# Grouping the small matrix products of a recurrent attention block, and lagging the values by half a unit

## The chip, the cores and the metric

The kernel runs on one core of one Trainium2 chip. The metric is the device time of the whole kernel in microseconds (us), from the first to the last instruction with what lies around them. All data are float32.

## The reference

A gated linear recurrence over 768 steps, for 4 batches and 8 heads of 48 channels, feeds a two-layer network with an ELU between its layers.

```python
mag = np.sqrt(a_re * a_re + a_im * a_im)
scale = np.minimum(mag, 0.999) / (mag + 1e-06)
a_re_n, a_im_n = (a_re * scale, a_im * scale)
for t in range(S):
    new_re = ar * S_re - ai * S_im
    new_im = ar * S_im + ai * S_re
    S_re, S_im = (new_re + kv, new_im)       # kv: outer product of k[t] and v[t]
    y[:, :, t] = einsum('bhd,bhde->bhe', q[:, :, t], S_re)
# x: y as (B*S, H*D) = (3072, 384)
h = x @ w_in                                  # 384 -> 2048
g = where(h > 0, h, exp(min(h, 0)) - 1)
out = g @ w_out                               # 2048 -> 384
```

## The kernel before: units, queues and a list written out by hand

The work is cut into 12 **units** (u = 0 to 11). A unit is 128 time steps of two batches; the two batches are its **halves** (n = 0, 1). Units u and u + 2 carry the same two batches on, so the state of one goes into the other. Inside a half the 128 steps are two chunks of 64.

A unit goes through these stages, each a function of the source:

- **Gates.** `squares`, `joined`, `logarithms`, `powers`, `lengths`, `ratios`, `slopes`, `angles`, `carried`, `noted` turn a_re and a_im into log magnitudes and angles on ScalarE (ACT), VectorE (DVE) and GpSimd (POOL). `decays` (`quartered`, L883) sums the logs over a chunk on TensorE (PE) and ACT takes six exponentials of them (L893). `turns` (L832) sums the angles on PE, four DVE operations (L837, L840) take off whole turns, `waves` makes sine and cosine with three ACT operations (L962, L965, L966), `scaled` multiplies q and k by the decays, `ends` fetches the chunk totals, and `gated` (L988) writes the gated q (DVE) and the gated k (POOL).
- **Small products.** For each half: `transposed` q and k (L1003 on PE, L1004 copies on ACT), `scores` (L1011, masked on DVE by L1016), `states` (L1039, then L1049 on DVE and L1051 on POOL for the running state), `values` (scores times v, L1061, then the carried state times q, L1068, then copies on ACT, L1076 and L1080). `seam` moves the rest of the values into place with DMAs of POOL's queue (L1093).
- **First layer.** `inner` (L1113) makes 256 columns of h in six products, which the trace shows as 12 matmuls of 128x128 by 256. `elu` follows: Relu (L1122) and Exp (L1123) on ACT, then L1124 on DVE. There are eight of each pair in a unit, written f = 0, 2, ... 14.
- **Second layer.** From unit 2 on it is 14 `product` calls (L1219, eight matmuls by 192 columns in the trace), a form of Strassen's scheme. `folded` (L1197, four DVE operations for each half of g) makes the combinations of g that it takes.

[...]

What sets the order: the code runs under a manual schedule. Each engine issues its instructions in the order in which the functions are called, and that is a list. The list `first` is written out to the end of unit 3 and some of unit 4's gates (down to `powers`, 4). After it come the calls made by `put(at, function, ...)`, sorted by `at`, and for equal `at` by the order in which they were put, that is by unit. A unit has SLOTS = 16 slots, and r = 16 (u - 2). Before the change, unit u loads at r + 8, has its gates from r + 11 to r + 19.5, its small products from r + 22 to r + 31, its eight `inner`/`elu` from r + 36 to r + 43 and its products from r + 44 to r + 52. So the gates and small products of unit u stand between the large products of units u - 1 and u - 2. A call that is in `first` already is not repeated. SP's queue issues the loads, the output stores and, every four slots, a `test_fetch` of weights (a DVE `test`, L680, follows it).

Of the kernel before, what the change touches and what calls it, by code (L numbers as in the profile page):

```python
# [10 lines left out]
FP32 = mybir.dt.float32  # L11
U32 = mybir.dt.uint32
AF = mybir.ActivationFunctionType
ALU = mybir.AluOpType
PSUM = bass.MemoryType.PSUM

C = 128
L = 64
# [487 lines left out]
def kernel(  # L506
# [12 lines left out]
    nc = tc.nc  # L519
    B, H, S, D = q.shape  # L520
    DM, DF = moe_w_in.shape[0], moe_w_out.shape[0]
    NI, NF = DM // C, DF // C
    NP = H // 2
    HD = H * D
    NB = 2
    NU = B // NB * (S // C)
# [10 lines left out]
    ps = ctx.enter_context(tc.tile_pool(name="ps", bufs=1, space=PSUM))  # L537
# [10 lines left out]
    def const(n, m, name):  # L548
        return cst.tile([n, m], FP32, name=name)
# [8 lines left out]
    G = HP - D  # L558
# [12 lines left out]
    def work(shape, tag="w"):  # L571
        return ps.tile(shape, FP32, tag=tag, bufs=3, name=tag)


    nat = [{} for _ in range(NU)]

    def where(u):
        return u % (B // NB) * NB, u // (B // NB) * C
# [107 lines left out]
    def flat(t):  # L686
        return t.rearrange("p n h d -> p (n h d)")
# [5 lines left out]
    def new(tag, bufs=1, shape=None):  # L693
        return sb.tile(shape or [C, NB, H, D], FP32, tag=tag, bufs=bufs, name=tag)
# [182 lines left out]
    def quartered(u):  # L877

        x = nat[u]
        both = [work([C, HD]) for n in range(NB)]  # L880
        for c in range(C // L):
            for n, t in enumerate(both):
                nc.tensor.matmul(  # L883
                    t[ts(c ^ n, L)], lhsT=sum_logs[ts(c, L), ts(c, L)],
                    rhs=flat(x["l"][ts(c, L), n : n + 1]), start=True, stop=True,
                )
        for n, t in enumerate(both):
            for key, sign in (("E", 1.0), ("F", -1.0)):
                pairs = [(slice(0, C), slice(0, C))]
                if n:  # L890
                    pairs = [(ts(c, L), ts(1 - c, L)) for c in range(C // L)]
                for to, of in pairs:
                    nc.scalar.activation(  # L893
                        out=flat(x[key][to, n : n + 1]), in_=t[of], func=AF.Exp, scale=sign
                    )
        ends = dram.tile([NB, C // L, H, D], FP32, tag="ends", bufs=2, name="ends")
        nc.scalar.dma_start(
            out=ends.rearrange("n c h d -> c n (h d)"),
            in_=x["E"][L - 1 :: L].rearrange("p n h d -> p n (h d)"),
        )  # L900
        x["ends"] = ends
# [11 lines left out]
    def decays(u):  # L913
        x = nat[u]
        if u > 1:
            x["E"], x["F"] = new("n", 6), new("n", 6)
            quartered(u)
            return
        for n in range(NB):
            x["sums", n] = work([C, HD])  # L920
            nc.tensor.matmul(
                x["sums", n], lhsT=sum_logs, rhs=x["l"][:, n].rearrange("p h d -> p (h d)"),
                start=True, stop=True,
            )
            decayed(u, n)
# [68 lines left out]
    state = {}  # L994
# [23 lines left out]
        )  # L1018

    def states(u, n):  # L1020

        x = nat[u]
        b, s = where(u)
        x["S", n] = [state.get(b + n)]
        if s == S - C:
            last = C // L - 1
        else:
            last = C // L
        gs = [
            work([C, H, D], "w" if u else "mlp") for c in range(last)  # L1030
        ]
        for h in range(H):
            for c, g in enumerate(gs):
                k = gates["k"][ts(c, L), n, h]
                parts = [(g[ts(i, HP), h], k[:, i]) for i in range(2)]
                if u == 0:
                    parts = [(g[:, h], k.rearrange("p i d -> p (i d)"))]
                for to, of in parts:
                    nc.tensor.matmul(  # L1039
                        to, lhsT=of, rhs=vn[u % 2][ts(c, L), n, ts(h, D)], start=True, stop=True,  # L1040
                    )
        for c, g in enumerate(gs):
            old = x["S", n][-1]
            new_s = new("S", 8, [C, H, D])
            wide = x["T"][:, n, c].unsqueeze(2).to_broadcast([C, H, D])
            if old is None:
                nc.vector.tensor_tensor(out=new_s, in0=g, in1=wide, op=ALU.mult)
            else:
                nc.vector.tensor_tensor(out=new_s, in0=g, in1=old, op=ALU.add)  # L1049
                eng = nc.vector if u < 2 else nc.gpsimd  # L1050
                eng.tensor_tensor(out=new_s, in0=new_s, in1=wide, op=ALU.mult)  # L1051
            x["S", n].append(new_s)
        state[b + n] = x["S", n][-1]

    def values(u, n):
        x = nat[u]
        y = ps.tile([C, C // L, 512], FP32, tag="y", bufs=1, name="y")
        each = [(p, c, j) for p in range(NP) for c in range(C // L) for j in range(2)]
        for p, c, j in each:

            nc.tensor.matmul(  # L1061
                y[ts(j, HP), c, ts(p, L)], lhsT=vn[u % 2][ts(c, L), n, ds((2 * p + j) * D, HP)],
                rhs=x["a", n][ts(c, L), 2 * p + j], start=(p == 0), stop=False,
                skip_group_check=True,
            )
        for p, c, j in each:
            if x["S", n][c] is not None:
                nc.tensor.matmul(  # L1068
                    y[ds(j * HP, D), c, ts(p, L)], lhsT=x["S", n][c][:, 2 * p + j],
                    rhs=x["qt", n][:, 2 * p + j, ts(c, L)], start=False, stop=False,  # L1070
                    skip_group_check=True,
                )
        if n == 0:
            x["x"], x["y"] = new("x", 2, [C, NI, GT]), new("y", 1, [C, GT])

        nc.scalar.copy(  # L1076
            out=x["x"][:, :, ts(n, C)].rearrange("p x (c t) -> p c x t", c=C // L),
            in_=y[:, :, 0 : NI * L].rearrange("p c (x t) -> p c x t", x=NI),
        )
        nc.scalar.copy(  # L1080
            out=x["y"][:, ts(n, C)].rearrange("p (c t) -> p c t", c=C // L),
            in_=y[:, :, NI * L : NP * L],
        )

    def seam(u):

# [166 lines left out]
    def verdict():  # L1253
# [31 lines left out]
        out=ident, in_=ident, pattern=[[-1, C]], base=0, channel_multiplier=1,  # L1285
# [6 lines left out]
    sum_turns, mask = const(C, C, "sum_turns"), const(C, L, "mask")  # L1292
# [35 lines left out]
    def put(at, fn, *args):  # L1328
        if fn is hidden:
            plan.append((at, len(plan), inner, args))  # L1330
            plan.append((at, len(plan), elu, args))
        else:
            plan.append((at, len(plan), fn, args))

    def decays_of(u, *at):
        fns = squares, logarithms, powers, lengths, ratios, slopes, noted, angles, carried
        put(at[0], begun, u)
        for x, fn in zip(at, fns):
            put(x, fn, u)
            if fn is squares:  # L1340
                put(x, joined, u)

    def gates_of(u, *at):
        for x, fn in zip(at, (decays, turns, waves, scaled, ends, gated)):
            put(x, fn, u)

    def values_of(u, *at):
        fns = (transposed, "q"), (transposed, "k"), (scores,), (states,), (values,)
        for n in range(NB):
            for x, (fn, *key) in zip(at[5 * n :], fns):  # L1350
                put(x, fn, u, *key, n)
        put(at[-1], seam, u)
# [72 lines left out]

    for u in range(2, NU):
        r = (u - 2) * SLOTS
        put(r + 8, load_a, u)
        put(r + 8, load_v, u)
        put(r + 8, load_qk, u)  # L1430
        if u == 2:
            decays_of(u, 16, 17, 17, 18.4, 19.5, 19.6, 22.7, 19.8, 19.8)
            gates_of(u, 20.4, 21.6, 22.1, 22.4, 22.4, 22.6)
        else:
            decays_of(u, r + 11, r + 12, r + 12, r + 13.4, r + 13.5, r + 14.9, r + 16.7, r + 15.5, r + 16.6)
            gates_of(u, r + 15, r + 18, r + 18.5, r + 18, r + 18, r + 19.5)
        values_of(u, *(max(r + 22, 24.5) + x for x in (0, 1, 2, 3, 5, 4, 5, 6, 7, 8, 9)))
        layer_of(u, range(r + 36, r + 44), range(r + 44, r + 52))
    for m in range(NR):
        put(40 + 4 * m, test_fetch, m)  # L1440
# [1 line left out]
    put(NU * SLOTS, verdict)  # L1442
    items = [(fn, tuple(args)) for fn, *args in first]
    items += [x[2:] for x in sorted(plan, key=lambda x: x[:2]) if x[2:] not in items]
    for fn, args in items:
        fn(*args)
    ctx.close()
# [35 lines left out]
```

## Time and profile before

| what | us |
|---|---|
| median of 3 runs | 699.82 (699.59 to 703.32) |
| span of the profiled execution | 700.0 |
| TensorE matmul busy | 674.0 |
| TensorE weight loads busy | 580.5 |
| ACT busy | 398.5 |
| DVE busy | 389.3 |
| POOL busy | 197.3 |

From about 216 us on PE shows no wait, and one unit follows another every 53.49 us (the first `inner` of a unit starts at 335.43, 388.91 and 442.40 us). In a timeline a line gives the start of a run of like instructions, its length, engine, line, operation, what is written from what, shape and count; the idle time before it and what ended that stand in brackets. The ends of matmuls are modelled and overlap the next line, so lengths on PE are read from start to start.

### The profile page before, as it was taken

To read this page: it belongs to the slowest core of one execution; us is meant where nothing else is said; L and a number is where in the kernel's file an instruction comes from. 1 tells how busy PE (TensorE), PEld (TensorE's weight loads), DVE (VectorE), ACT (ScalarE), POOL (GpSimd) and SP (SyncE) were. 2 spreads that over 40 slices of the span, in tenths; PEclk is the share of its full clock that TensorE was granted. 3 is DMA by queue.
4 is the path that set the end of the run, shared out by engine and by line. 5 is a ranking of instruction groups with operands and counts; after the bars stand their busy time and mean duration, and the time that the engine had idled before them with its cause. 6 is when DMAs were issued, how large, how long until landed. Compare 5 with 4: busy or idle time off the path is not lost.

```text
span 700.0 us, 15771 instructions
## 1 busy us (share of the span) xinstructions
PE 674.0 (96%) x6656; PEld 580.5 (83%) x6656; DVE 389.3 (56%) x579; ACT 398.5 (57%) x630; POOL 197.3 (28%) x207
## 2 busy tenths in 40 slices
PE   8799899997999999999999999999999999999996
PEld 6687786575788889888988989889888988989995
DVE  5888999814757544554553553553554644642151
ACT  6774445748656764765655656657557547541230
POOL 2000000115514414414415415406407305402000
PEclk9979999999999999999999999999999999999999
DMA  9995756152082911821921821831731631100000
GB/s 169 175 150 83 144 176 165 17 103 64 3 137 63 143 50 38 138 43 50 136 48 53 123 61 52 121 63 53 108 75 53 123 62 52 47 1 8 23 1 28
DMA packets 149899, 55.98 MB, mean 80 GB/s; under 512 B 129172, under 2 KB 142652, under 8 KB 149820
## 3 DMA queue, kind: packets, MB, share of 16 engines
q1 hardware_dynamic: 146240, 53.53, 40.6%
q0 software_dynamic: 3360, 1.22, 1.3%
q8 instruction: 54, 0.88, 0.5%
q14 instruction: 25, 0.20, 0.1%
q10 hardware_dynamic: 220, 0.14, 0.1%
HBM read 48.88 MB, written 4.78 MB: 77 GB/s over the span
## 4 chain that ended last, share of the span: by engine, by line
PE 85%; DVE 4%; SPq 3%; ACT 2%; DMA 2%; issue 2%; POOL 1%; ACTq 0%; POOLq 0%; DVEq 0%
PE mlp L1113 33%; PE mlp L1219 26%; PE w L1003 5%; PE mlp L1134 4%; PE w L1011 3%; PE y L1068 3%; PE w L1039 3%; SPq L596 2%; PE y L1061 2%; PE w L832 2%; PE w L1134 1%; PE w L883 1%; DMA w<-in_moe_w_in_dram 1%; DMA w<-in_a_im_dram 1%; POOL kg L988 1%
## 5 line engine op out<-in xcount | busy, mean ns | idle before, releaser
L1113 PE MATMUL mlp<-x,w_in 128*128 128x256 f32 x1152 | 262.9, 383 | 2.9 <-DVE g L1124 2.9
L1113 PEld LDWEIGHTS mlp<-x,w_in 128*128 128x128 f32 x1152 | 215.8, 191 | 32.5 <-DVE g L1124 3.3
L1124 DVE SCALAR_TENSOR_TENSOR g<-ee,mlp 128x512 f32<-128x512 f32 x96 | 65.6, 685 | 116.6 <-ACT ee L1123 111.0
L1122 ACT ACTIVATE ee<-mlp 128x512 f32<-128x512 f32 x96 | 57.3, 596 | 127.6 <-PE mlp L1113 118.7
L1219 PE MATMUL mlp<-w_out,g 128*128 128x192 f32 x640 | 111.1, 328 | 0.0
L1219 PEld LDWEIGHTS mlp<-w_out,g 128*128 128x128 f32 x640 | 104.3, 190 | 2.8
L1051 POOL TENSOR_TENSOR S<-S,T 128x384 f32<-128x384 f32 x36 | 29.9, 831 | 163.7 <-DVE S L1049 163.7
L1123 ACT ACTIVATE ee<-ee 128x512 f32<-128x512 f32 x96 | 60.5, 630 | 2.9
L1197 DVE TENSOR_TENSOR g<-g 128x512 f32<-128x512 f32 x80 | 56.8, 711 | 2.7
L1219 PE MATMUL mlp<-w,g 128*128 128x192 f32 x320 | 56.9, 332 | 0.0
L1219 PEld LDWEIGHTS mlp<-w,g 128*128 128x128 f32 x320 | 51.6, 190 | 5.8 <-issue 4.8
L856 POOL DMA_DIRECT2D carry<-n x10 | 5.0, 501 | 142.0 <-DVE n L840 142.0
L988 POOL TENSOR_TENSOR kg<-k,cs 128x1536 f32<-128x1536 f32 x9 | 38.8, 4309 | 18.4 <-issue 18.4
L1093 POOL DMA_DIRECT2D x<-y x65 | 31.8, 496 | 42.7 <-ACT y L1080 42.7
L1049 DVE TENSOR_TENSOR S<-w,S 128x384 f32<-128x384 f32 x38 | 21.1, 556 | 40.7 <-PE w L1039 25.4
L893 ACT ACTIVATE n<-w 64x384 f32<-64x384 f32 (+1 forms) x60 | 28.1, 486 | 22.7 <-PE w L883 22.0
L1238 ACT COPY o<-mlp 128x192 f32<-128x192 f32 x10 | 3.2, 319 | 64.6 <-DMA out_dram<-o 42.9
L716 POOL TENSOR_TENSOR n<-n 128x768 f32<-128x768 f32 x9 | 16.4, 1819 | 66.9 <-ACT n L710 66.9
L1134 PE MATMUL mlp<-w_out,g 128*128 128x384 f32 x96 | 32.9, 490 | 0.7 <-DVE g L1124 0.7
L1004 ACT COPY qt<-w 128x512 f32<-128x512 f32 x48 | 25.5, 584 | 11.9 <-PE w L1003 11.9
L1011 PEld LDWEIGHTS w<-qt,kt 128*64 128x64 f32 x768 | 24.4, 137 | 7.9 <-issue 4.5
L988 DVE TENSOR_TENSOR qg<-q,cs 128x1536 f32<-128x1536 f32 (+1 forms) x12 | 19.5, 1623 | 19.2 <-ACT cs L966 19.2
(165 smaller groups left out, 992.3 us busy)
## 6 DMA issues: line engine op xcount, KB each, us to landing
w<-in_moe_w_out_dram SPq DMA_DIRECT2D x8, 768.0 KB
g<-in_moe_w_in_dram SPq DMA_DIRECT2D x16, 384.0 KB
g<-in_moe_w_out_dram SPq DMA_DIRECT2D x16, 384.0 KB
w<-in_moe_w_in_dram SPq DMA_DIRECT2D x16, 288.0 KB
vn<-in_v_dram SPq DMA_DIRECT2D x24, 192.0 KB
out_dram<-o SPq DMA_DIRECT2D x48, 96.0 KB
ar<-in_a_re_dram SPq DMA_DIRECT2D x22, 192.0 KB
ai<-in_a_im_dram SPq DMA_DIRECT2D x22, 192.0 KB
```

The source lines that it names most:

```text
L988: eng.tensor_tensor(out=to[:, :, :, 0:D], in0=each.unsqueeze(2).to_broadcast([C, step * H, 2, D]), in1=x["cs"][:, n * H : (n + step) * H], ...
L1003: nc.tensor.transpose(t[:, h], of, ident)
L1011: nc.tensor.matmul(t[ts(c, L), h], lhsT=x["kt", n][:, h, ts(c, L)], rhs=x["qt", n][:, h, ts(c, L)], start=True, stop=True,)
L1051: eng.tensor_tensor(out=new_s, in0=new_s, in1=wide, op=ALU.mult)
L1093: eng.dma_start(out=x["x"][ds(j * HP + D, G), i], in_=x["y"][ds(j * HP + i * G, G)])
L1113: nc.tensor.matmul(t[:, e], lhsT=w_in[:, i, ts(f + e, C)], rhs=x["x"][:, i], start=(i == 0), stop=(i == NI - 1),)
L1122: nc.scalar.activation(out=e, in_=t, func=AF.Relu, scale=-1.0)
L1123: nc.scalar.activation(out=e, in_=e, func=AF.Exp, scale=-1.0)
L1124: nc.vector.scalar_tensor_tensor(out=x["g", f // 8][:, f % 8 : f % 8 + 2], in0=e, scalar=-1.0, in1=t, op0=ALU.add, op1=ALU.max)
L1134: nc.tensor.matmul(x["o", n], lhsT=x["g", f // 8][:, f % 8, ts(n, C)], rhs=w_out[:, f], start=(f == 0), stop=(f == NF - 1),)
L1197: nc.vector.tensor_tensor(out=S_of(u, k, h), in0=a, in1=b, op=op)
L1219: nc.tensor.matmul(to, lhsT=a[:, m], rhs=b[:, m], start=(first and h == 0 and m == 0), stop=False, skip_group_check=True,)
```

## The change

From unit 4 on (`LONE = 4`):

- `states` and `values` are cut into their products and the rest (`state_products`, `state_sums`, `value_products`, `carried_products`, `value_copies`); the instructions are the same.
- `piece(u, n)` issues as one run: the log sums of unit u + 1 (for n = 1), value products of the half before, state products of this half, carried products of the half before, and scores of this half. After that come the state sums, the value copies of the half before and the mask of the scores.
- The scores are written to columns 256 to 511 of the two "y" banks, whose first 256 columns hold the values. One of the two banks of the log sums comes from "mlp" for u > 4.
- A unit's loads of a, q and k and its gates stand 8.5 slots earlier, its transposes and small products likewise: transposes from r + 13.5 and r + 21.2, pieces at r + 17 and r + 24.7. The values of n = 1 come with the first piece of the next unit, at r + 33, and `seam` after it. The first layer stays at r + 36.

```diff
-        both = [work([C, HD]) for n in range(NB)]
+        both = [work([C, HD], "mlp" if n and u > LONE else "w") for n in range(NB)]
...
+    LONE = 4
+
+    def piece(u, n):
+
+        u0, n0 = (u, 0) if n else (u - 1, 1)
+        half = H // 2
+        x = nat[u] if u < NU else None
+        if n and u + 1 < NU:
+            decays(u + 1)
+        y = ps.tile([C, C // L, 512], FP32, tag="y", bufs=1, name="y")
+        if u0 >= LONE:
+            value_products(u0, n0, y)
+        if x:
+            state_products(u, n)
+        if u0 >= LONE:
+            carried_products(u0, n0, y)
+        if x:
+            for h in range(H):
+                for c in range(C // L):
+                    nc.tensor.matmul(
+                        y[ts(c, L), h // half, ds(256 + h % half * L, L)],
+                        lhsT=x["kt", n][:, h, ts(c, L)], rhs=x["qt", n][:, h, ts(c, L)],
+                        start=True, stop=True, skip_group_check=True,
+                    )
+            state_sums(u, n)
+        if u0 >= LONE:
+            value_copies(u0, n0, y)
+        if x:
+            x["a", n] = new("a", 2, [C, H, L])
+            shape = [C, 2, half, L]
+            nc.vector.tensor_tensor(
+                out=x["a", n].rearrange("p (z h) t -> p z h t", z=2),
+                in0=y[:, :, 256:512].rearrange("p z (h t) -> p z h t", t=L),
+                in1=mask.unsqueeze(1).unsqueeze(1).to_broadcast(shape), op=ALU.mult,
+            )
...
     def gates_of(u, *at):
         for x, fn in zip(at, (decays, turns, waves, scaled, ends, gated)):
-            put(x, fn, u)
+            if fn is not decays or u <= LONE:
+                put(x, fn, u)
...
-        put(r + 8, load_a, u)
-        put(r + 8, load_v, u)
-        put(r + 8, load_qk, u)
+        b = r if u < LONE else r - 8.5
+        put(b + 8, load_a, u)
+        put(r + 8 if u < LONE else r + 4, load_v, u)
+        put(b + 8, load_qk, u)
...
-            decays_of(u, r + 11, r + 12, r + 12, r + 13.4, r + 13.5, r + 14.9, r + 16.7, r + 15.5, r + 16.6)
-            gates_of(u, r + 15, r + 18, r + 18.5, r + 18, r + 18, r + 19.5)
-        values_of(u, *(max(r + 22, 24.5) + x for x in (0, 1, 2, 3, 5, 4, 5, 6, 7, 8, 9)))
+            decays_of(u, b + 11, b + 12, b + 12, b + 13.4, b + 13.5, b + 14.9, b + 16.7, b + 15.5, b + 16.6)
+            gates_of(u, b + 15, b + 18, b + 18.5, b + 18, b + 18, b + 19.5)
+        if u < LONE:
+            values_of(u, *(max(r + 22, 24.5) + x for x in (0, 1, 2, 3, 5, 4, 5, 6, 7, 8, 9)))
+        else:
+            for n, at in enumerate((r + 13.5, r + 21.2)):
+                put(at, transposed, u, "q", n)
+                put(at + 1.5, transposed, u, "k", n)
+                put(at + 3.5, piece, u, n)
+            put(r + 33, piece, u + 1, 0)
+            put(r + 33, seam, u)
```

The list `first` is not touched. By the sort rule, the calls that follow it for unit 4 are, after the change: `load_qk`, `load_v`, `lengths`, `ratios`, `slopes`, `decays`, `angles`, `carried`, `noted`, `turns`, `scaled`, `ends`, `waves`, `folded` (2, 1), `gated`, `transposed` q, and then `product` (2, 4, 1). For a later unit, say 6, the calls around its gates are: `inner` (4, 10), `elu`, `turns` 6, `scaled`, `ends`, `inner` (4, 12), `elu`, `waves` 6, `inner` (4, 14), `elu`, `folded` (4, 1), `gated` 6, three `product` of unit 4, `transposed` q of 6.

More of the change, by code (lines that the diff above doesn't have):

```diff
@@ L1020, in states, with state_products @@
     def states(u, n):
+        state_products(u, n)
+        state_sums(u, n)
+    def state_products(u, n):
         x = nat[u]
@@ L1028, in states @@
             last = C // L
-        gs = [
+        x["G", n] = gs = [
             work([C, H, D], "w" if u else "mlp") for c in range(last)
@@ L1041, in states, with state_sums @@
                     )
-        for c, g in enumerate(gs):
+    def state_sums(u, n):
+        x = nat[u]
+        for c, g in enumerate(x["G", n]):
             old = x["S", n][-1]
@@ L1052, in states, with value_products @@
             x["S", n].append(new_s)
-        state[b + n] = x["S", n][-1]
+        state[where(u)[0] + n] = x["S", n][-1]
     def values(u, n):
+        y = ps.tile([C, C // L, 512], FP32, tag="y", bufs=1, name="y")
+        value_products(u, n, y)
+        carried_products(u, n, y)
+        value_copies(u, n, y)
+    EACH = [(p, c, j) for p in range(NP) for c in range(C // L) for j in range(2)]
+    def value_products(u, n, y):
         x = nat[u]
-        y = ps.tile([C, C // L, 512], FP32, tag="y", bufs=1, name="y")
-        each = [(p, c, j) for p in range(NP) for c in range(C // L) for j in range(2)]
-        for p, c, j in each:
+        for p, c, j in EACH:
             nc.tensor.matmul(
@@ L1065, in values, with carried_products @@
             )
-        for p, c, j in each:
+    def carried_products(u, n, y):
+        x = nat[u]
+        for p, c, j in EACH:
             if x["S", n][c] is not None:
@@ L1072, in values, with value_copies @@
                 )
+    def value_copies(u, n, y):
+        x = nat[u]
         if n == 0:
@@ L1083, in values @@
         )
+    LONE = 4
[5 more added lines that the diff above has]
+            decays(u + 1)
+        y = ps.tile([C, C // L, 512], FP32, tag="y", bufs=1, name="y")
+        if u0 >= LONE:
+            value_products(u0, n0, y)
+        if x:
+            state_products(u, n)
+        if u0 >= LONE:
[8 more added lines that the diff above has]
+                    )
+            state_sums(u, n)
+        if u0 >= LONE:
[8 more added lines that the diff above has]
+            )
     def seam(u):
@@ L1444 @@
     items += [x[2:] for x in sorted(plan, key=lambda x: x[:2]) if x[2:] not in items]
+    items = [x for n, x in enumerate(items) if x[0] is not piece or x not in items[:n]]
     for fn, args in items:
```

## The prediction

> **What bounds the kernel now.** I read the page first (busy shares, the 40 slices, the chain's shares).
>
> ```profile
> PE 674.0 (96%) x6656; PEld 580.5 (83%) x6656; DVE 389.3 (56%) x579; ACT 398.5 (57%) x630; POOL 197.3 (28%) x207
> ...
> PE   8799899997999999999999999999999999999996
> ...
> PE 85%; DVE 4%; SPq 3%; ACT 2%; DMA 2%; issue 2%; POOL 1%; ACTq 0%; POOLq 0%; DVEq 0%
> ```
>
> PE is full from the eleventh slice on, and the chain is PE's own instructions. So only two things can move the end: PE's work itself, or a hole in PE's stream. Next the timeline of PE inside a unit, to see what a small group costs between large ones, and one older place where two groups stand together:
>
> ```profile
> 401.02 2.75 PE L1113 MATMUL mlp<-x,w_in 128*128 128x256 f32 x12
> 403.71 1.15 PE L1011 MATMUL w<-qt,kt 128*64 128x64 f32 x32
> 404.79 2.86 PE L1113 MATMUL mlp<-x,w_in 128*128 128x256 f32 x12
> 407.58 1.15 PE L1039 MATMUL w<-vn,kg 64*64 64x48 f32 x64
> ...
> 185.73 1.15 PE L1039 MATMUL w<-vn,kg 64*64 64x48 f32 x64
> 186.81 1.15 PE L1011 MATMUL w<-qt,kt 128*64 128x64 f32 x32
> 187.89 5.45 PE L1113 MATMUL mlp<-x,w_in 128*128 128x256 f32 x24
> ```
>
> Start to start, 12 matmuls of L1113 take 2.59 us undisturbed (a run of 36 takes 7.77). Ahead of a small group they take 2.69 (401.02 to 403.71), between two 2.79. So each small group costs 0.1 us on either side, 0.2 in all; transposes cost none. At 185.73 two groups stand together, take 1.08 each as ever, and have one pair of edges.
>
> Then the timelines of ACT and DVE around the gates, since the change moves them:
>
> ```profile
> 387.73 1.28 ACT L962 ACT_TABLE_LOAD   x1
> 389.02 0.84 ACT L962 ACTIVATE cs<-n 128x768 f32<-128x768 f32 x1
> ...
> 391.70 0.60 ACT L1122 ACTIVATE ee<-mlp 128x512 f32<-128x512 f32 x1
> 392.32 1.28 ACT L1123 ACT_TABLE_LOAD   x1
> 393.61 0.63 ACT L1123 ACTIVATE ee<-ee 128x512 f32<-128x512 f32 x1
> ```
>
> ```profile
> 391.60 1.76 DVE L988 TENSOR_TENSOR qg<-q,cs 128x1536 f32<-128x1536 f32 x1 [1.81 <-ACT cs L966]
> ...
> 402.36 2.87 DVE L1197 TENSOR_TENSOR g<-g 128x512 f32<-128x512 f32 x4
> ```
>
> `waves` holds ACT for 3.97 us (387.73 to 391.70), table load included; the next `elu` takes 3.26 from its Relu to the end of its L1124 (394.96), since it must load Exp's table again. `gated` q then needs 1.76 and `folded` 2.87 on DVE. None of it shows on PE today: `turns` ends at 385.01 and the transpose of q begins at 396.68, with three products and three `inner` between.
>
> [...]
>
> **The change, part by part.**
>
> *Grouping.* Before, units 4 to 11 have six small groups each (scores, states, values, twice) and seven log sums for units 5 to 11: 55 groups. After, there are 16 pieces and a last one of values alone: 17. 38 groups fewer x 0.2 = 7.6 us; the first half's values stood before a transpose and had only about 0.15, so 8 x 0.05 comes off: **-7.2 us**, all on PE and so on the path. Inside a piece the counts and shapes are the same; whether order within a piece gains or costs isn't in the trace, +-0.1 us for each of 17, +-1.7; I take 0.
>
> *Score banks and copies.* Copies and mask now share banks and may wait for each other, but the next user of "y" is half a unit away: 0. If that cover went, it would be one 0.75 us copy pair a piece. The log sums' bank from "mlp" is free after the six exponentials, about 2.9 us, and is wanted three allocations (over 5 us of PE) later: 0. SP: loads move ahead of stores and `test_fetch`; q and k are free once the gates before are made: 0. `seam`: six POOL issues of 0.49 and 1.7 to land, behind two L1051, end about 9.5 us after the piece begins; `inner` follows about 10.5 after: 0, by 1 us.
>
> *Unit 4's gates.* `first` still ends with `powers` 4 and is followed after the change by unit 4's whole gate chain, and no PE work stands in it. PE is in order, so it waits three times. The times on either side are from this trace:
>
> ```profile
> 214.75 0.96 DVE L772 SCALAR_TENSOR_TENSOR n<-n 128x768 f32<-128x768 f32 x1 [0.44 <-ACT n L746]
> ...
> 221.84 0.94 DVE L821 SCALAR_TENSOR_TENSOR n<-carry,n 1x768 f32<-1x768 f32 x1 [1.11 <-ACT n L815]
> ```
>
> Product (2, 4, 0) ends at 210.36; L883 still can't start before 215.86, after L772: 5.5 us. L883 ends at 216.67; `turns` needs L821, ended at 222.78: 6.2. `turns` ends at 224.2; DVE then has `noted` to 224.5, L837/L840 2.4, `scaled` 0.95, `folded` 2.87, `gated` q 1.76, so the transpose starts at 232.5: 8.3. Sum 20.0, less the 1.1 that PE waits there today: **+18.9 us**.
>
> *Gates of units 5 to 11.* They move from among the second layer's products to among the first layer's `elu`. From the end of `inner` f = 12 (E): its `elu` leaves ACT at E + 1.37 (411.35 to 412.72 in the trace). `waves` 3.97: E + 5.34. `elu` f = 14 queues behind it, 3.26: E + 8.6. `folded` is put ahead of `gated` (same slot, earlier unit), 2.8: E + 11.4. `gated` q 1.76 and a tenth to PE: E + 13.3. The angles are no later: DVE has them at E + 0.7. PE meanwhile has `inner` 14 (2.59) and three products (1.30 each): 6.49, then comes the transpose. Hole: **6.8 us** in each of 7 units, **+47.6**. (The third product also reads f = 14's result, so some 2.5 of the 6.8 falls ahead of it.) Queued behind the waiting transpose are all of PE's later products, and behind those ACT and DVE: the hole repeats each unit.
>
> *Clock.* The page's windows show what a low stretch does:
>
> ```profile
> 50.00:55.00 5.00, 5.00 (x15) 3.71 (x15) 3.52 (x6) 1.44 (x2) 0.00 (x0) 0.67 1.17 175
> ```
>
> There 12 matmuls of L1113 take 4.4 us for 2.6, +1.8. How PE answers a hole of 6.8 us with a third of a microsecond of work in it isn't in this trace: [...] I take one dip of 1.8 for unit 4 and each of 7 units: **+14.4**.
>
> **Sum** against the profiled 700.0 (median 699.8): 700.0 - 7.2 + 18.9 + 47.6 + 14.4 = 773.7; I say **773**.
>
> **Rivals.**
> (a) *Holes without dips*: 759. For it: the 2.9 us wait that left the clock alone. Against: holes here are twice that.
> (b) *Faster: the grouping alone decides.* If PE's transpose is never late, 7.2 us come off: 693. It takes that the gate chain from E needs under 6.5 us and not 13.3, and that unit 4's chain has other PE work beside it. For it: PE is 96% busy with ACT and DVE at 57 and 56%, so on average there is room. Against: averages don't help a chain of 13.3 us beside 6.5 of work, and the order is fixed by the list. It decides from the point where `waves` and `gated` would both run ahead of `elu` 14 and `folded`.
> (c) *Only unit 4 pays* (the later units' chain hidden): 700.0 - 7.2 + 18.9 + 1.8 = 713. For: before, the same chain was hidden with 3.3 us to spare (gated q ends at 393.36, its transpose begins at 396.68). Against: E + 13.3.
> (d) *More waits than I see*, say another 2 us a unit since ACT carries six table loads a unit instead of five and lags into the next `inner`: about 790.
>
> **How the numbers follow.** 773 has 0.60, (a) 0.18, (b) 0.07, (c) 0.06, (d) 0.09. A measurement tells about 0.5% (3.5 us) from no change. Faster takes (b), with a little left for no change: 0.07 faster, 0.02 same, 0.91 slower. The range 748 to 790 takes in (a), most of (d), the dips from 0 to 2 x 1.8 and the 1.7 on the order within a piece; (b) and (c) stay out, 0.13.
>
> **What would show it.** Unit period before the end: 53.5 - 1 + 6.8 + 1.8, about 61 us. PE's L1003 on qg should wait some 4 us on DVE L988 in each of units 5 to 11, and L1219 some 2.5 on DVE L1124; the busy slices of PE fall to about 9 and 8. At unit 4 PE should stand near 5.5, 6.2 and 8.3 us ahead of L883, L832 and L1003. Between large groups, edges of 0.2 only twice a unit. I am wrong if PE's row stays full of nines beyond the first third: then the chain was hidden; or if the waits fall elsewhere, on `inner` or on SP.

## The result and the profile after

The kernel after takes **781.65 us** (median of 4 runs, 779.42 to 784.13), the kernel before 699.71 (4 runs, 699.01 to 703.32): a ratio of 1.116 with a 95% interval of 1.113 to 1.120. The profiled execution spans 780.0 us, against 700.0 before, at a mean granted clock of 0.937 against 0.989. An execution that takes over 1.5% longer than the fastest of the same kernel, as one of `waves_after_elu` further down, is left out of every reading. The lines of the page that answer to the first three of before:

```profile
PE 685.1 (88%) x6656; PEld 599.0 (77%) x6656; DVE 395.8 (51%) x579; ACT 405.7 (52%) x636; POOL 192.4 (25%) x207
...
PE   8898999989718987996996996996996998899996
...
PE 68%; DVE 12%; ACT 11%; SPq 2%; DMA 2%; issue 2%; POOL 1%; ACTq 0%; POOLq 0%; DVEq 0%
```

The number of matmuls is unchanged, but PE's row is no longer full of nines. A deep gap stands at the eleventh and twelfth slice (unit 4), and then a 6 comes back every third slice, roughly a unit's period (slices of 9 and 8 were forecast). DVE and ACT, together 6% of the chain before, are now 23% of it. So PE no longer sets the end alone; it waits for them. In the waits of PE, each row is what it waited for, then the sum in us, how often, and the longest. The first two rows are:

```profile
PE w L1003 <- DVE qg L988: 45.1, 9, 12.9
PE mlp L1273 <- DVE g L1178: 15.3, 7, 2.2
```

Lines have moved: L1273 is the old L1219 (`product`), L1178 the old L1124 (end of `elu`), L1167 the old L1113 (`inner`), L1251 the old L1197 (`folded`). Seven waits of 2.2 us stand ahead of a second-layer product and seven of 3.8 to 4.8 ahead of the transposes of gated q; the longest of the first row, 12.9, is in unit 4. In the timeline of PE, a later unit looks like this (start, duration, instruction, and in brackets the idle time and what ended it):

```profile
473.45 1.14 PE L1273 MATMUL mlp<-w_out,g 128*128 128x192 f32 x6
476.78 0.59 PE L1273 MATMUL mlp<-w_out,g 128*128 128x192 f32 x2 [2.19 <-DVE g L1178]
482.13 1.97 PE L1003 MATMUL w<-ident,qg 128*128 128x128 f32 x8 [4.75 <-DVE qg L988]
483.89 2.77 PE L1273 MATMUL mlp<-wt,g 128*128 128x192 f32 x8
486.45 2.93 PE L1273 MATMUL mlp<-w,g 128*128 128x192 f32 x16
```

From the start of one such transpose to the next are 61.46 us (482.13 to 543.59; 60.9 to 62.2 in the other units), against a period of 53.49 before. A hole is time in which PE stands. With 0.163 us for an undisturbed matmul of L1273 (2.60 for 16), the two holes are 2.36 and 5.03 us, 7.4 in all; they are the same in units 5 to 9, and 6.8 in units 10 and 11. After them the 8 transposes take 1.76 start to start (0.87 elsewhere) and the next 8 matmuls of L1273 2.56 (1.30 elsewhere). That is half the clock, which the table of windows shows as well (the seventh column after the window is the granted clock):

```profile
482.00:484.00 2.00, 1.87 (x9) 1.88 (x10) 0.54 (x2) 0.59 (x1) 0.00 (x0) 0.50 0.18 48
484.00:487.00 3.00, 3.00 (x12) 3.00 (x12) 0.00 (x0) 0.59 (x1) 0.00 (x0) 0.54 0.91 225
487.00:490.00 3.00, 3.00 (x23) 2.98 (x22) 0.51 (x2) 0.15 (x1) 0.00 (x0) 1.00 1.42 189
```

Unit 4, in the same timeline of PE:

```profile
212.60 1.56 PE L883 MATMUL w<-n,sum_logs 64*64 64x384 f32 x8 [5.32 <-DVE n L772]
220.35 2.90 PE L832 MATMUL w<-n,sum_turns 128*128 128x384 f32 x4 [6.19 <-DVE n L821]
236.14 1.97 PE L1003 MATMUL w<-ident,qg 128*128 128x128 f32 x8 [12.90 <-DVE qg L988]
```

These are the three waits that were forecast, in their order; the third is half as long again, and all three groups run at half clock (granted 0.50 in the table of windows from 212 to 215, from 220 to 223 and from 236 to 238 us; L832 takes 2.90 for 1.45). The timelines of DVE and, below, of POOL show why the third is long:

```profile
225.22 9.20 DVE L1251 TENSOR_TENSOR g<-g 128x512 f32<-128x512 f32 x4
234.34 1.75 DVE L988 TENSOR_TENSOR qg<-q,cs 128x1536 f32<-128x1536 f32 x1
...
476.76 3.64 DVE L1251 TENSOR_TENSOR g<-g 128x512 f32<-128x512 f32 x4
```

```profile
225.28 1.82 POOL L976 TENSOR_TENSOR k<-k,n 128x768 f32<-128x768 f32 x1
...
228.97 3.44 POOL L988 TENSOR_TENSOR kg<-k,cs 128x1536 f32<-128x1536 f32 x1
...
474.23 3.44 POOL L988 TENSOR_TENSOR kg<-k,cs 128x1536 f32<-128x1536 f32 x1
```

`folded` is four adds of 0.69 us each, 2.87 in all where the prediction read it. In unit 4 it takes 9.20 and in a later unit 3.64: each time POOL is at work on `scaled` or `gated` k, and an add that is caught ends about half a microsecond after POOL's instruction does (POOL's kg ends at 232.41, the second add of unit 4 at 232.97; in the later unit they end at 477.67 and 478.23).

### The profile page after: what moved, and what is told of

Same layout as the page of the kernel before. It is cut to its first block, busy times and chain, and to the rows that moved or that the text cites. A ratio compares the mean times of both kernels' runs of the same rounds, so it can differ in the third digit from the quotient of the medians.

```text
span 780.0 us, 15763 instructions
## 1 busy us (share of the span) xinstructions
PE 685.1 (88%) x6656; PEld 599.0 (77%) x6656; DVE 395.8 (51%) x579; ACT 405.7 (52%) x636; POOL 192.4 (25%) x207
## 4 chain that ended last, share of the span: by engine, by line
PE 68%; DVE 12%; ACT 11%; SPq 2%; DMA 2%; issue 2%; POOL 1%; ACTq 0%; POOLq 0%; DVEq 0%
PE mlp L1167 26%; PE mlp L1273 22%; PE w L1003 5%; DVE g L1251 4%; PE y L1083 3%; PE w L1043 2%; PE y L1122 2%; DVE qg L988 2%; SPq L596 2%; PE w L832 2%; PE mlp L1188 2%; PE y L1074 1%; ACT L962 1%; ACT ee L1177 1%; DVE g L1178 1%
## 5 line engine op out<-in xcount | busy, mean ns | idle before, releaser
L1167 PE MATMUL mlp<-x,w_in 128*128 128x256 f32 x1152 | 260.9, 382 | 2.7 <-DVE g L1178 2.4
L1167 PEld LDWEIGHTS mlp<-x,w_in 128*128 128x128 f32 x1152 | 217.0, 191 | 34.7 <-DVE g L1178 2.8
L1178 DVE SCALAR_TENSOR_TENSOR g<-ee,mlp 128x512 f32<-128x512 f32 x96 | 65.4, 684 | 139.0 <-ACT ee L1177 138.9
L1273 PE MATMUL mlp<-w_out,g 128*128 128x192 f32 x640 | 114.0, 330 | 15.3 <-DVE g L1178 15.3
L1273 PEld LDWEIGHTS mlp<-w_out,g 128*128 128x128 f32 x640 | 104.8, 191 | 18.6 <-DVE g L1178 17.4
L1003 PE MATMUL w<-ident,qg 128*128 128x128 f32 x192 | 32.8, 326 | 45.7 <-DVE qg L988 45.1
L1251 DVE TENSOR_TENSOR g<-g 128x512 f32<-128x512 f32 x80 | 67.6, 845 | 2.7
L1003 PEld LDWEIGHTS w<-ident,qg 128*128 128x128 f32 x192 | 27.2, 168 | 51.9 <-DVE qg L988 49.1
L1273 PE MATMUL mlp<-w,g 128*128 128x192 f32 x320 | 58.2, 338 | 0.0
L1273 PEld LDWEIGHTS mlp<-w,g 128*128 128x128 f32 x320 | 56.6, 203 | 0.0
L1056 DVE TENSOR_TENSOR S<-w,S 128x384 f32<-128x384 f32 x38 | 21.0, 553 | 70.1 <-PE w L1043 54.8
L1004 ACT COPY kt<-w 128x512 f32<-128x512 f32 x48 | 25.7, 587 | 48.4 <-PE w L1003 48.4
L1094 ACT COPY x<-y 128x384 f32<-128x384 f32 x24 | 11.5, 478 | 64.3 <-PE y L1122 49.9
L1273 PE MATMUL mlp<-wt,g 128*128 128x192 f32 x160 | 39.7, 406 | 0.0
L1285 DVE TENSOR_TENSOR ee<-mlp,ee 128x192 f32<-128x192 f32 x10 | 3.6, 358 | 63.4 <-PE mlp L1273 63.4
L1273 PEld LDWEIGHTS mlp<-wt,g 128*128 128x128 f32 x160 | 35.7, 249 | 0.0
L988 POOL TENSOR_TENSOR kg<-k,cs 128x1536 f32<-128x1536 f32 x9 | 32.5, 3613 | 8.8 <-issue 5.7
```

The costliest lines, as they stand in the source:

```text
L988: eng.tensor_tensor(out=to[:, :, :, 0:D], in0=each.unsqueeze(2).to_broadcast([C, step * H, 2, D]), in1=x["cs"][:, n * H : (n + step) * H], ...
L1003: nc.tensor.transpose(t[:, h], of, ident)
L1004: nc.scalar.copy(out=o[:, h0 : h0 + 4], in_=t)
L1167: nc.tensor.matmul(t[:, e], lhsT=w_in[:, i, ts(f + e, C)], rhs=x["x"][:, i], start=(i == 0), stop=(i == NI - 1),)
L1178: nc.vector.scalar_tensor_tensor(out=x["g", f // 8][:, f % 8 : f % 8 + 2], in0=e, scalar=-1.0, in1=t, op0=ALU.add, op1=ALU.max)
L1251: nc.vector.tensor_tensor(out=S_of(u, k, h), in0=a, in1=b, op=op)
```

## The experiments

All times are medians; a ratio is to the kernel before on the same chip, with its 95% interval. The first four and `folded_ahead` change the kernel after; `scores_by_states` and the two `grouped_in_place` change the kernel before; `regrouped` and `regrouped_split` go from after back towards before in their order. Where times of different rows, or of after (781.65), are set against each other, the kernel before differs by up to 2.4 us between the sets of runs.

| kernel | us | kernel before | ratio |
|---|---|---|---|
| gated_before_elu | 742.03 | 701.83 | 1.058 (1.049 to 1.066) |
| waves_after_elu | 742.75 and 760.05 | 701.83 | none |
| unit4_spread | 764.13 | 701.83 | 1.089 (1.078 to 1.101) |
| holes_filled | 773.30 | 701.83 | 1.102 (1.093 to 1.111) |
| folded_ahead | 775.52 | 700.44 | 1.108 (1.104 to 1.111) |
| regrouped | 707.47 | 700.44 | 1.010 (1.008 to 1.012) |
| regrouped_split | 719.74 | 700.44 | 1.029 (1.027 to 1.032) |
| scores_by_states | 696.44 | 700.44 | 0.995 (0.993 to 0.997) |
| grouped_in_place | 700.37 | 700.15 | 1.0005 (0.9989 to 1.0022) |
| grouped_in_place_later | 702.33 | 702.13 | 1.0008 (0.9995 to 1.0021) |

My theory was that of the prediction: the order of the list puts a chain of ACT and DVE between `inner` and the transposes, and PE, in order, stands. The rivals were that the holes alone count and not the clock, and that the group itself is what costs.

**gated_before_elu** puts `gated` of the later units ahead of `folded` in the queue of DVE.

```diff
-            gates_of(u, b + 15, b + 18, b + 18.5, b + 18, b + 18, b + 19.5)
+            gates_of(u, b + 15, b + 18, b + 18.5, b + 18, b + 18, b + (19.5 if u <= LONE else 19.4))
```

> The changed kernel with one call moved: for units 5 to 11 the gated q and k are put just ahead of the last inner and elu of the unit before last (slot b + 19.4 for 19.5), so on DVE ahead of L1178 for f = 14 and of folded. Theory of the queue order: gated q is then done 7.1 us after the end of inner 12, against 6.5 us of PE work, so the wait of 4.8 us ahead of the transposes goes; the wait of 2.2 us inside the third product stays, since elu 14 still stands behind waves on ACT. Seven units give back 7 x 4.8 = 33 us, and up to 7 x 2.3 = 16 more if the clock no longer dips: 732 to 748 us. Rival, that the holes come with the pieces themselves (banks of y shared by scores, values and mask): nothing changes, about 781 us.

Measured: 742.03, some 40 us less than after. The wait of the transposes on `gated` q is gone from units 5 to 11 (in four of them a wait of 0.5 to 1.0 us for a copy of ACT comes instead, ahead of the k transposes); that of L1273, 2.19 us, is left, since `waves` still stands ahead of the last `elu` on ACT. A tenth of a slot in the list was worth half of the loss.

**waves_after_elu** takes the other part of the chain away: `waves` and `gated` come after the last `elu` of the unit.

```diff
-            gates_of(u, b + 15, b + 18, b + 18.5, b + 18, b + 18, b + 19.5)
+            z = 0 if u <= LONE else 1
+            gates_of(u, b + 15, b + 18, b + 18.5 + z, b + 18, b + 18, b + 19.5 + 0.1 * z)
```

> The changed kernel with waves (and gated after it) of units 5 to 11 put behind the last elu and folded instead of between the last two elu. Theory of the queue order: elu 14 no longer waits for the sines nor loads Exp's table anew, so the wait of 2.2 us inside the third product goes; the sines end about 8.0 us after inner 12 and gated q at 9.8, against 6.5 us of PE work, so one wait of 3.4 us ahead of the transposes is left in place of 2.2 + 4.8. Seven units give back 7 x 3.7 = 26 us, up to 42 if the clock dips less: 740 to 756 us. Rival, that it is the number of table loads or ACT's load as such and not the order: one load less for a unit is 1.3 us, 7 x 1.3 = 9, about 772. Rival of the shared banks: about 781.

Measured: two executions, 742.75 and 760.05, of which only the first, the profiled one, is read. One hole a unit is left, in the timeline of PE:

```profile
462.00 1.09 PE L1003 MATMUL w<-ident,qg 128*128 128x128 f32 x8 [3.20 <-DVE qg L988]
```

The wait of L1273 is gone and the other is 3.20 us in each of the seven units, for 3.4 expected.

**unit4_spread** gives unit 4 the slots that it had before, and keeps the rest of the change.

```diff
-        b = r if u < LONE else r - 8.5
+        b = r if u <= LONE else r - 8.5
...
-            for n, at in enumerate((r + 13.5, r + 21.2)):
-                put(at, transposed, u, "q", n)
-                put(at + 1.5, transposed, u, "k", n)
-                put(at + 3.5, piece, u, n)
+            for n, (tq, tk, at) in enumerate(
+                ((22, 23, 24), (25, 25.1, 25.3)) if u == LONE else ((13.5, 15, 17), (21.2, 22.7, 24.7))
+            ):
+                put(r + tq, transposed, u, "q", n)
+                put(r + tk, transposed, u, "k", n)
+                put(r + at, piece, u, n)
```

(Unit 5's loads of a, q and k are put at 48.8 and 51.6 as well.)

> The changed kernel with unit 4's gates back where they were before the change (among the products of unit 2) and its transposes and two pieces put into the first layer of unit 3; unit 5's loads of a, q and k moved behind unit 4's last use of those buffers. All later units as in the changed kernel. Theory: the three waits of 5.3, 6.2 and 12.9 us and the half clock around them go, some 27 us: about 754 us. If unit 4's start were hidden by what follows (PE catches up later), it stays at 775 or more.

Measured: 764.13, so 10 us too many. The three waits are gone (of the first, the 1.1 us of the kernel before are back), but a new one stands in the timeline of PE, and it brings a half-clock stretch of its own (12 matmuls in 5.28 us for 2.59; the slice of the page from 229 to 248 us is granted 0.7):

```profile
243.28 5.49 PE L1167 MATMUL mlp<-x,w_in 128*128 128x256 f32 x12 [6.32 <-DVE g L1178]
```

Where unit 4 is late and unit 5 early, both gate chains meet on ACT: unit 4's `waves` and unit 5's squares, logs and exponentials hold ACT from 230.2 to 241.3, and the first `elu` of `inner` is queued behind them. So unit 4's hole is more than a slip of one unit's slots: two units' gates stand close together wherever in the list the step of 8.5 slots is put. That is read from the list; only the places of this run and of `regrouped` were tried.

**holes_filled** lets PE run 40 unneeded matmuls in the longer hole, to keep its clock up.

```diff
+            if u > LONE:
+                put(r + 13.45, warm, 20)
```

> The changed kernel with 20 products of the identity with itself (128 x 128, results unused) put on PE just ahead of the q transposes of units 5 to 11, some 4.3 us of work into the wait of 4.8. They add work that nobody needs and fill the hole. If the slow transposes and products after a hole (1.97 us for 1.04, 5.3 for 3.9) are the clock, granted at 0.5 there, they go back to their usual lengths and each unit gets 2.3 us shorter though PE has more to do: 7 x 2.3 = 16, about 765 us. If they are slow for another reason (a cold start of the pipeline, copies or banks), the time stays at 781 or rises.

Measured: 773.30, 8.4 us below after. In the timeline of PE, in unit 8:

```profile
475.40 6.25 PE L1376 MATMUL mlp<-ident 128*128 128x128 f32 x40
481.50 1.04 PE L1003 MATMUL w<-ident,qg 128*128 128x128 f32 x8
```

The transposes behind the fill take 1.04 again, not 1.97, and in none of the seven units is the work behind it slow. But the fill itself isn't the same everywhere. In the chain that ended last (start, length, engine, what, count), units 8 and 9 have:

```profile
475.57 6.09 PE mlp L1376 x40
536.29 4.46 PE mlp L1376 x40
```

The 4.46 us, the some 4.3 that were expected, are found in three units; in the other four the same 40 matmuls take 6.09. The 1.63 us between them are, by an estimate, 3.3 us at half clock, as much as a low hole of 2.19 us brings in gated_before_elu (further down). So I take it that the same hole, which is left ahead of the fill, lowers the clock in four units, and there the fill overruns the hole that it was to fill by 1.1 to 1.7 us. From the first to the last of the seven waits of L1273, which is six units, it takes 361.4 us, for 369.8 in after: the 15.3 us that the slow work behind the holes cost in after are gone, the fills take back 4.8, and short stalls elsewhere some 2. The profiled execution is granted 0.961 in the mean, for 0.937 in after. So what is slow behind a hole is the clock, and the rival of holes without dips is out.

**folded_ahead** tests the surprise of unit 4: `folded` of unit 2 is put earlier in DVE's queue, ahead of L780 of unit 4.

```diff
-        put(at_h[7], folded, u, 1)
+        put(at_h[7] if u > 2 else 36.95, folded, u, 1)
```

> The changed kernel with the one folded call that stands in unit 4's gate chain (unit 2, second half) put ahead of that chain, where DVE is idle. The same four operations took 9.2 us there, while GpSimd was multiplying k, against 2.8 elsewhere. If that time is on the path, the third wait of unit 4 falls from 12.9 to some 5.5 us: 781 - 7 = 774 us. If GpSimd then blocks the gated q in the same way, little or nothing is gained: 779 to 782.

Measured: 775.52, 6.1 us less. The third wait of unit 4 fell from 12.9 to 5.6, and the second rose from 6.2 to 7.1. `folded` ahead of `gated` had cost 7.3 there and not 2.87. At its new place it takes 5.96, beside two other multiplies of POOL (L759, L760).

**regrouped** keeps the groups and mends the order: `waves` and `gated` after the last `elu` and `folded`, the transposes a little later, unit 4 spread, and unit 5's gates at slots of their own.

```diff
-            gates_of(u, b + 15, b + 18, b + 18.5, b + 18, b + 18, b + 19.5)
+            z = 0 if u <= LONE else 1
+            gates_of(u, b + 15, b + 18, b + 18.5 + z, b + 18, b + 18, b + 19.5 + 0.1 * z)
...
+                ((22, 23, 24), (25, 25.1, 25.3)) if u == LONE else ((15.45, 16.1, 17), (21.2, 22.7, 24.7))
```

> The pieces of the changed kernel with an order in which nothing should be late. Units 6 to 11: waves and gated behind the last elu and folded, and the first half's q and k transposes two to three products later, so that q has 11.7 us of PE work (inner 14 and seven products) beside a chain of 9.9, and k some 13.9 beside 13.4. Unit 4: gates among the products of unit 2 as before the change, its transposes and pieces in the first layer of unit 3. Unit 5: its logarithms behind elu 6 of unit 3 and its turns and gates behind inner 14. If the holes were the order of the queues and grouping is worth what the changed kernel's trace shows (a unit's own PE work 1.7 us less), it ends at 700 - 8 x 1.7 = 686 us, some 3 more if the start of unit 4 and 5 keeps a hole: 684 to 692. If grouping is worth only the edges that I had counted (0.9 us a unit): 693. If pieces themselves bring waits (the rival): 700 or more.

Measured: 707.47. The period of a later unit did come down to 52.26 us (301.63 to 353.89), 1.2 below before, so grouping as such isn't what costs. But the passage through units 4 and 5 lost some 14 to 15 us, by an estimate: the profiled span is 8.4 us above before, and the periods after it save some 6. PE waits there for L1056 (3.3 and 1.8 us), for L821 (1.7) and for a copy on ACT (4.0), and runs slowly behind L1056 and the copy (8 transposes take 1.97 us for 1.04, 24 matmuls of L1273 6.74 for 3.90; the two slices of the page from 248 to 283 us are granted 0.8). My expectation failed on that passage, not on the period.

**regrouped_split** cuts each piece of units 5 to 11 into five runs apart from each other, everything else as in regrouped.

```diff
-                put(r + at, piece, u, n)
+                for i, at in enumerate(((13.4, 14.6, 16.7, 17, 17.2), (20.5, 22.3, 23.5, 24.5, 25.3))[n]):
+                    if n or i != 3:
+                        put(r + at, part, u, n, i)
```

> As the run before (regrouped), but for units 5 to 11 the pieces are taken apart again: values, carried products, states, log sums and scores are issued at five places of a half, with large products or transposes between, on the same banks and with the same lag. Nine small groups a unit instead of two. If a group costs only its two edges of 0.2 us, this is 7 x 1.4 = 10 us slower than regrouped; if groups that stand together also overlap (0.3 us a piece in the trace), 15 us slower, near the 699.8 of before. If grouping did nothing, the same time.

Measured: 719.74, 12.3 above regrouped, between the two expectations. The passage through units 4 and 5 differs too, so the periods are the better reading: 54.58 (515.02 to 569.60) against 52.26, and without a wait of 0.67 in the one and of 0.37 in the other about 53.9 against 51.9. Nine runs instead of two are 7 x 0.2 = 1.4 us of edges; some 0.6 is left. That fits what the kernel after shows in its own timeline of PE, where some groups that stand together also overlap:

```profile
494.08 0.69 PE L1074 MATMUL y<-a,vn 64*64 64x64 f32 x32
494.60 1.10 PE L1043 MATMUL w<-vn,kg 64*64 64x48 f32 x64
495.63 1.10 PE L1083 MATMUL y<-qt,S 128*48 128x64 f32 x32
496.56 1.10 PE L1122 MATMUL y<-qt,kt 128*64 128x64 f32 x32
497.59 6.77 PE L1273 MATMUL mlp<-w_out,g 128*128 128x192 f32 x40
```

The piece takes 3.51 us (494.08 to 497.59); in the kernel before, the four take 0.63, 1.08, 1.03 and 1.08 from start to start, 3.82. The 0.3 is saved at two of the three borders, 0.15 at each: between the two groups of 64*64 (0.52 for 0.63, and 1.03 for 1.08), and between 128*48 and 128*64 (0.93 for 1.03, and 1.03 for 1.08). At the border from 64*64 to 128*48, where the rows of the tile change from 64 to 128, nothing is saved. The trace of grouped_in_place, further down, has the same lengths at the same kinds of border (0.93 and 1.03 for 128*48 and 128*64; 0.62 for 64*64 ahead of 128*48).

**scores_by_states** is the smallest grouping: in the kernel before, scores and states of a half share a slot. Shown is only the list of slots of `values_of`: for each half transposed q, transposed k, scores, states and values, and last `seam`.

```diff
-(0, 1, 2, 3, 5, 4, 5, 6, 7, 8, 9)
+(0, 1, 2, 2, 5, 4, 5, 6, 6, 8, 9)
```

> The kernel before with one thing changed: the states of each half of units 4 to 11 are issued right behind the scores, without the one large group between them. 16 boundaries fewer at 0.2 us: 3.2 us off the kernel before, 696.6. If a boundary costs nothing (the 0.2 is how the trace models ends), no difference.

Measured: 696.44, 4.0 us below before. The period is 53.09, 0.40 less: two pairs of edges of 0.2. The gain is small, 0.5%, but its interval (0.993 to 0.997) is clear of 1. This is the one version that beats both kernels.

**grouped_in_place** goes further with the same means: values of one half join scores and states, those of the other join the log sums.

```diff
-(0, 1, 2, 3, 5, 4, 5, 6, 7, 8, 9)
+(0, 1, 2, 2, 6, 4, 5, 6, 6, 8.95, 9)
```

> The kernel before with grouping alone, and no gate moved: for units 4 to 11 the values of the first half wait for the scores of the second and stand together with them and its states, the states of the first half stand behind its scores, and the values of the second half stand next to the next unit's log sums. Three small groups a unit instead of seven. Theory (a group costs two edges of 0.1 us, and groups that stand together overlap by another 0.1 to 0.3 us a unit): 8 x (0.8 + 0.1 to 0.3) = 7 to 9 us less than the kernel before, about 692. Rival, that the values' lag or the shared place makes PE wait (for a mask, a copy or a bank): 697 or more, with waits on L1061 or L1011.

Measured: 700.37, no gain. The timeline of PE shows a wait in each of 7 units that the kernel before doesn't have:

```profile
371.52 2.87 PE L1219 MATMUL mlp<-w,g 128*128 128x192 f32 x16 [0.70 <-ACT ee L1227]
```

The product needs the PSUM bank (one of the buffers that the matmuls are written to) that ACT's copy L1227 reads, and that copy (ended at 371.47) is queued behind a block of logs. In the kernel before, values stood between the products and gave ACT the time.

**grouped_in_place_later** moves the group of the second half behind two products, to give that copy its time.

```diff
-(0, 1, 2, 3, 5, 4, 5, 6, 7, 8, 9)
+(0, 1, 2, 2, 7.9, 4, 5, 7.9, 7.9, 8.95, 9)
```

> As grouped_in_place, with the middle group (values of the first half, scores and states of the second) two products later, behind product (4, 1). In grouped_in_place each of seven units lost 0.7 us where product (6, 0) waited for a copy of ACT (L1227) out of the bank that it writes; the copy stands behind six microseconds of logarithms, and the small groups had been the work that covered it. With the group between product (4, 1) and (6, 0), 3.7 us of work cover it again. If that wait is why grouping gave nothing, the time is now 8 x 0.9 = 7 us less than the kernel before: 692 to 694. If grouping itself gives nothing here, 700.

Measured: 702.33, no gain again. The wait on the copy shrinks to 0.24, and another takes its place:

```profile
376.24 0.99 PE L1068 MATMUL y<-qt,S 128*48 128x64 f32 x28 [0.66 <-POOL S L1051]
```

The carried products need POOL's state sum L1051, which begins at 375.36 only. In the chain that ended last, POOL has ahead of it:

```profile
371.67 1.85 POOL n L759
373.59 1.81 POOL n L760
```

These are multiplies of the next unit's gates. In the kernel before, the states come earlier and their sums stand ahead of the two (423.29 and 424.79, then L759 at 425.75). So once more it is the order in another engine's queue. In both kernels the edges that are saved come back as a wait of about the same size.

## Why the prediction was right, and where it was off

The direction, the place and the mechanism were right: 773 forecast, 781.65 measured. But errors go against each other in that sum: holes, clock and unit 4 came out 14.5 us larger than forecast, the grouping and the start 8.2 lower, so that the total is as near as it is partly by luck. Term by term, against the profiled executions (700.0 and 780.0):

| term | forecast | measured | from |
|---|---|---|---|
| start, the same code in both | 0 | -3.3 | the last product ahead of unit 4's first wait ends at 210.36 and 207.12 |
| unit 4, waits, less the 1.1 of before | +18.9 | +23.3 | 5.3 + 6.2 + 12.9 - 1.1 |
| unit 4, clock and the rest | +1.8 | +3.5 | remainder, with what grouping saves in unit 4 |
| units 5 to 11, holes | +47.6 | +50.6 | 7.4 in units 5 to 9, 6.8 in 10 and 11 |
| units 5 to 11, clock | +12.6 | +18.0 | 2.3 to 3.0 a unit |
| grouping | -7.2 | -12.1 | 7 x (53.49 + 7.38 + 2.31 - 61.46) |

The first row is no effect of the change: in after, gated_before_elu, waves_after_elu and holes_filled, whose code is the same up to there, L883 of unit 4 starts at 212.60, 214.74, 212.83 and 215.53.

**The holes.** The step "from the end of `inner` f = 12" was right in each part: both waits are on the lines that it names, 2.19 and 4.75 us for "some 2.5" and "some 4". gated_before_elu and waves_after_elu each take one part of that chain out of PE's way and give back some 40 us. The mis-sized term is `folded`: 2.8 forecast, 3.64 measured (3.12 in units 10 and 11).

**Unit 4.** Its first two waits were 5.5 and 6.2 in the forecast and are 5.3 and 6.2. The third was forecast at 8.3 with `folded` at 2.87, and is 12.9 with `folded` at 9.20. Both misses on `folded` are one omission: I took its duration from a place where POOL was idle and never asked what POOL does at the new place. The traces show that the two collide: the four adds in unit 4 take 2.44, 5.28, 0.7 and 0.7 us, and folded_ahead gets 6.1 us back by moving them. In later units the first add takes the longer, the more of POOL's kg is left when it begins: 0.94 us where 0.39 are left (units 10 and 11), 1.47 where 0.91 are (unit 8). In the kernel before POOL is the one held up: kg begins at 392.71, while gated q has DVE until 393.36, and takes 3.97 us, for 3.44 in the kernel after. One part isn't explained so: the two long adds of unit 4 begin, by their records, 0.06 and 1.3 us ahead of the multiply that they end behind, the second while POOL issues two DMAs. No run took POOL's multiplies away by themselves, and what the two engines compete for is in no trace.

**The clock.** One dip of 1.8 a unit was forecast from one low stretch; that a hole brings one such dip was an estimate, which the trace of before doesn't show. It is 2.3 in unit 8 (0.89 at the transposes, 1.26 and 0.16 at the 8 and 16 matmuls behind them) and up to 3.0 in the others, 2.6 in the mean; holes_filled shows that it is the clock. In unit 4 I took one dip for three waits: L883 and L832 show 0.7 and 1.5 us lost to half clock, the transposes and the products behind them 2.4.

**The grouping.** The gain was larger than forecast. The edges come to -0.95 a later unit: 7 x 0.2 less 0.05 before, 2 x 0.2 after. The order inside a piece, for which I took 0 with bounds of +-0.1, is worth 0.3 us in the piece shown (3.51 for 3.82) and 0.45 in the one with the log sums, some 0.75 a unit: 0.15 for each border between small groups whose tiles have the same rows. That is outside the bounds. Together -1.7, as measured. The prediction's own sample of two groups side by side (185.73) is 64*64 beside 128*64, where the rows change, so the saving couldn't be seen there.

**The rivals.** Holes without dips (759) falls with holes_filled. The grouping alone (693) and only unit 4 (713) fall with the two rows of waits that recur seven times. Of more waits than forecast (790) nothing is seen: no other wait of PE recurs in each unit. The excess over 773 is in the size of the terms. That the first `inner` after a piece would wait for SP or for `seam` isn't seen in the waits of PE.

What stays open: how much could be had from the full group with a passage through units 4 and 5 that doesn't stall. A period of 52.26 for 53.49 over 7 units would be 8.6 us below before; no version here had the period and the passage together.

## What to carry to other kernels

When a step is moved in a fixed order, write out the queue of every engine at its new place, and price each instruction there with what the neighbouring engines do at that time: the chain behind a move (here 13.9 us, from the end of `inner` f = 12 at 468.27 to the transposes at 482.13, beside 6.5 us of PE's work) counts for more than the edges that it saves. Small groups that stand spread between large ones may be the cover of another engine's latency, so grouping them can only be gained where that latency is covered by something else. Group first what is ready at the same time and stands close together already: that gave 0.5% here, and the further groups none.

## What was not expected of the hardware

**A hole of 2 to 3 us can halve the clock, or not.** The hole of gated_before_elu recurs in each of units 5 to 11 with 2.19 us. In its table of windows, the stretch around the hole of one unit is granted 0.79, and that of the next 1.00; two of the seven are low:

```profile
348.00:356.00 8.00, 6.90 (x35) 6.86 (x36) 5.70 (x6) 1.81 (x4) 3.00 (x1) 0.79 0.06 12
404.00:412.00 8.00, 6.99 (x47) 6.76 (x48) 6.06 (x7) 2.62 (x6) 2.92 (x1) 1.00 0.06 12
```

In waves_after_elu the hole of 3.20 us has it the other way round, 1.00 in the first of these windows and 0.79 in the second; three of the seven are low. By an estimate, 0.79 over 8 us is a stretch of some 3.4 us at half clock (0.21 x 8 x 2); behind the other low hole of gated_before_elu the four microseconds from 462 to 466 are granted 0.57. So the same hole does it in one unit and not in the next, and 2.19 us of idleness were enough. Nor does a longer one always do it: the kernel before waits 2.88 us ahead of 79.01, and is granted 1.00 from 76 to 84 us. What decides is in no trace. In the kernel after, where the holes come to 6.8 to 7.4 us with a third of a microsecond of work in them, the clock falls in every one of the 7 units: the 2.5 us behind the start of each unit's transposes are granted 0.50.

**Neighbouring small groups overlap where their tiles have the same rows**, by 0.15 us a border in the piece of the kernel after (64*64 beside 64*64, 128*48 beside 128*64), beyond the 0.2 us that each pair of edges to large groups costs; from 64*64 to 128*48, where the rows change, nothing is saved. **DVE's add of two SBUF tiles** of 128x512 takes 0.69 us alone, and up to 5.28 when POOL is at work.
